# Outputs of nine chunks from ScalarE copies to a head's own half, without a drain, and a new order list

## The chip, the cores and the metric

The kernel runs on one NeuronCore of a Trainium2 chip. The metric is the device time of one execution in microseconds (us). Five engines work side by side, each through its own queue in order: TensorE (PE in the profile; its weight loads are PEld), VectorE (DVE), ScalarE (ACT), GpSimd (POOL) and SyncE (SP), whose queue issues nearly all DMAs here. They meet at semaphores.

## The reference

Two blocks follow each other. The first is a delta rule over a sequence, per batch and head; the second a feed-forward product of three matrices.

```python
B, H, S, D = 4, 8, 768, 48
k_n = k / (norm(k) + 1e-6)
for t in range(S):
    y[:, :, t] = einsum('bhd,bhde->bhe', q[:, :, t], state)
    v_old = einsum('bhde,bhd->bhe', state, k_n[:, :, t])
    state = state + beta_t * einsum('bhd,bhe->bhde', k_n[:, :, t], v[:, :, t] - v_old)
x = y.transpose(0, 2, 1, 3).reshape(B * S, H * D)      # 3072 x 384
out = (((x @ w1) * (x @ w2)) @ w3) @ w_out             # 384 -> 1024 -> 1024 -> 384
```

All of it is computed in fp32; the weights come in as 64-bit numbers and are converted on the chip.

## The kernel before

**The first block in chunks.** The 768 steps are cut into 12 chunks of 64 tokens. Two batches lie in the two halves of the 128 partitions (z = 0, 1), the other two in r = 0, 1; heads come in even and odd (e = h % 2). For a chunk m the steps are:

- `p`, `d` (or `K`, `Q` for chunks 0 and 1): keys and queries with features on the partitions, in the tile KQ; an even head's features lie in partitions 0 to 47, an odd head's in 64 to 111.
- `s`, scores, per r (a "half" of the scores): products of keys with keys and queries into a pair of PSUM banks, ps_w. VectorE takes the key part as U; the query part becomes PT, by a ScalarE copy and a GpSimd mask (chunks 0, 1 and 4 to 11), or by one VectorE product (chunks 2 and 3).
- `u`, `V`, `e`: the triangular inverse of U, for two chunks at a time. `V` is 31 steps of two VectorE operations each, with its matrix held in one pair of PSUM banks; before and behind it stand copies or DMAs, and `e` puts the corner block in.
- `c`, the chain: state times keys (from chunk 1 on), vtok minus that, the inverse times vtok, then X on VectorE (L685), then the new state S. Only this part is sequential from chunk to chunk.
- `y`, outputs: state times queries plus X times PT in one pair of PSUM banks, eight ScalarE copies into xT (L765), and every second chunk DMAs within xT.

In X and PT the data of head h and batch half z lie in partition half (z + h) % 2: odd heads are crossed. So the scores put an odd head's query part into the other half than its key part, with two products of 64 columns (L387), where an even head has one of 128 (L381). The outputs run in two modes: state products of z = 0 and all X times PT products, then `pe.drain()`, then state products of z = 1. The PSUM bank of a product is (h + z) % 2.

**The second block.** Per pair of chunks (u = 0 to 5) the feed-forward products run as `a h i j` (L988, for pair 0 `a b` at L869), sums on GpSimd (`G`, `S`), and the last product as `o` with results `x` (L1098, L1128 to L1135, stores at L1115). w3 and w_out are multiplied together at the start (`t`, `f`), after each weight piece is loaded and converted (`P`: DMA, ScalarE, VectorE, GpSimd).

**Buffers.** `two_banks()` hands out the two pairs of ps_w in turn; while an inverse `V` holds one, every other user gets the other. Tag "o" has two buffers, which the squares of the keys (`g`) and the result tiles (osb) take in turn.

**Order.** Each part is a generator and each `yield` a step. ORDER is a list of some 1,460 names written out by hand; every occurrence of a name runs that part's next step. The instructions of each engine keep the order in which they were emitted, so the list fixes all five queues.

Of the kernel before, what the change touches and what calls it, by code (L numbers as in the profile page):

```python
# [39 lines left out]
V0 P0 k0 beta P18 P13 P0 P18 P0 P0 P11 g0 P13 K0 P18 K0 P11 P18 P10 P13 P13 q0 P3 P3 P11 g0 beta  # L40
beta K0 K0 K0 k1 K1 P10 P11 P12 P3 P12 g0 g0 Q0 P10 g0 g0 g0 g0 g0 P8 Q0 Q0 Q0 K1 K1 K1 Q0 K1 P3
N0 P9 k2 P8 P8 P10 s0 P8 N0 g1 s0 s0 s0 s0 s0 s0 u0 q1 P2 Q1 P9 p2 P2 P12 P12 P9 Q1 g1 Q1 Q1 P2
u0 g1 Q1 d2 d2 u0 P5 P1 t0 t0 t5 t5 P9 t2 t2 P4 P6 s1 s1 P5 P5 P2 s1 P1 s1 s1 s1 u1 g1 P1 u1 u1
t4 V0 V0 P5 V0 V0 P4 t10 P7 P4 t3 t3 V0 V0 P1 f1 P6 P6 t4 V0 P7 V0 V0 t10 t1 P14 P7 P4 V0 f0 V0
P6 P16 P16 V0 V0 P7 t1 s0 P19 P19 P19 P19 V0 f1 P17 k3 p2 v1 V0 V0 P14 P14 P14 V0 f2 P17 f2 f0 V0
f2 P15 v0 P20 f1 t11 f0 P17 P17 f5 V0 V0 P16 t11 P16 t8 P15 V1 V0 t8 f5 t9 V0 V0 t6 P15 V0 n0 n0
f5 V0 V0 V0 V0 t9 P20 P20 V0 t6 P22 P22 P22 f4 P23 P23 V0 f4 f4 P21 P21 P15 t7 t7 V0 s1 V0 V0 V0
V0 g1 d2 d2 P22 f3 f3 P24 P20 g1 g1 p3 g1 P26 p3 P30 e0 e0 e0 t12 t14 e1 e1 g1 f3 e0 e0 d3 d3 N1
s2 s2 s2 P23 P23 t12 e0 f6 e0 p4 s2 P24 e1 e1 t14 s2 e0 P24 s2 P25 c0 P26 f7 u2 P30 P24 c0 e1 e1
P21 P21 d3 d3 y0 y0 P26 P26 P31 t15 t13 s3 s3 s3 s3 s3 s3 t13 c0 n1 n1 P32 t15 u2 u2 u3 c0 P30 f7  # L50
e1 P25 P25 P31 P31 P27 c1 c1 u3 u3 f6 e1 c1 V1 V1 V1 y0 P31 f6 f7 P25 P27 V1 V1 V1 V1 P30 b1 c1
N1 b1 v2 P32 V1 V1 P27 V1 s1 y1 y1 b2 V1 d4 V1 V1 P28 P29 P32 b2 P27 V2 V1 V1 V1 y1 b3 V1 V1 P28
P28 b0 P32 c1 b2 b2 b3 b1 b1 b0 P29 P29 b0 P29 a03 a03 a02 V1 b0 V1 d4 V1 V1 a01 V1 P28 V1 V1 a02
V1 P35 a01 a00 a00 n2 n2 a04 a04 b7 P33 P33 a05 a05 P34 P34 a01 a07 b7 V1 b4 b5 V1 V1 V1 V1 k4
a01 a07 k5 b5 b3 g2 b4 V1 V1 P35 V1 V1 g2 c1 e2 e2 e2 e2 a06 a06 g2 e3 e3 e3 b3 g2 g2 a00 a02 a02
p4 v3 d4 d4 p5 a00 e2 P34 c2 c2 e2 P34 e2 b6 P35 P35 e2 c2 c2 e3 a03 g2 g2 P33 b6 y2 g2 P33 g2 d5
d5 p5 c2 c2 y2 a04 e3 s4 N2 e3 s4 a03 s4 b6 b6 s4 s4 s4 s4 T e3 T T d5 n3 d5 a04 e3 b4 b4 b7 s5
n3 k6 g3 u4 s5 s5 s5 s5 s5 s5 b5 b7 b5 a05 T c3 c3 a06 a05 a06 u5 V2 p6 g3 a07 a07 c3 c3 g3 S0 S0
S0 V2 g3 V2 V2 N2 oD0 y3 y3 V2 V2 W oA0 S0 S0 V2 V2 S0 S0 S0 c3 v5 n5 V2 V2 S0 S0 S0 S0 V2 v4 oB0
V2 V2 V2 xA0 V2 V2 xB0 V2 V2 oA0 S0 S0 S0 n4 oB0 xA0 d6 y3 k7 xA0 V2 n4 oC0 V2 V2 V2 a10 xB0 S0  # L60
V2 V2 xC0 G1 V2 xD0 a10 a10 V2 oC0 a10 a10 d6 xC0 xC0 xC0 xD0 V2 V2 i10 V2 h10 c3 c4 V2 V2 j10 V2
V2 V2 a10 h10 i10 a12 V2 V2 h10 W W a12 p6 V2 a12 a12 j12 e4 g3 g3 h10 c4 a12 h10 a12 h12 d6 d6
s5 i12 e4 e4 e4 i10 h12 h12 g3 g3 p7 g3 e4 e4 h12 N3 s4 h12 a11 a11 a11 s6 s6 i12 i12 e5 c4 j11
s6 c4 y4 y4 c4 e5 d7 d7 h11 c4 c5 a11 p7 e5 s6 a11 a11 h11 i11 i11 n5 c5 d7 d7 N3 a13 h11 h11 e5
W e5 s7 e5 a13 s7 s7 s7 s7 s7 s7 a13 a13 s6 s6 c5 i11 k8 u7 u6 g4 g4 g4 S1 V3 V3 c5 p8 h11 s6 g4
h13 a13 j13 a13 i13 h13 i13 i13 S1 h13 V3 h13 h13 V3 V3 y5 V3 V3 V3 V3 V3 V3 d8 V3 V3 V3 y5 oC1
oA1 S1 oD1 S1 S1 V3 V3 S1 xA1 c5 oA1 xA1 oB1 v6 y5 v7 a20 a20 V3 xA1 V3 V3 V3 d8 G2 V3 V3 xB1 n6
V3 V3 V3 V3 oB1 xB1 xC1 S1 j20 k9 V3 xD1 V3 V3 V3 V3 S1 oC1 a20 a20 p8 xC1 V3 xC1 h20 V3 xD1 xC1
V3 V3 V3 V3 a20 a20 i20 h20 a22 h20 g4 c5 g4 g4 g4 a22 V3 j22 d8 h20 h20 e6 i20 g4 a22 d8 a22 h22
a22 a22 i22 e6 V4 e6 c6 i20 h22 e6 i22 h22 n7 h22 e6 e6 a21 a21 a21 n6 c6 p9 c6 s8 i22 N4 h21 h22  # L70
i21 a21 s8 a21 s6 c6 y6 s8 s8 j21 s8 v8 a21 h21 i21 y6 d9 d9 e7 p9 e7 s8 s8 e7 e7 s7 h21 h21 i21
h21 a23 c6 c6 e7 a23 i23 a23 n8 n8 d9 e7 S2 N4 d9 a23 s9 s9 s9 s9 s9 n7 s9 k10 s9 u8 g5 a23 a23
c7 c7 h23 h23 i23 i23 c7 c7 g5 u9 h23 h23 V4 V4 V4 j23 h23 S2 g5 g5 V4 V4 V4 V4 p10 v9 V4 y7 y7
V4 V4 oA2 V4 V4 d10 V4 y7 V4 V4 S2 oD2 S2 d10 xA2 V4 S2 S2 oB2 oC2 V4 c7 xB2 V4 V4 V4 V4 oB2 xB2
xC2 xD2 p10 V4 V4 V4 oA2 V4 V4 a30 a30 G3 a30 a30 S2 S2 oC2 k11 V4 xC2 j30 s9 V4 xD2 xC2 V4 V4 V4
V4 V4 V4 xA2 xA2 xC2 g5 a30 h30 a30 i30 a32 h30 V4 V4 V4 e8 h30 i30 c7 a32 j32 h30 h30 g5 a32 a32
i32 g5 g5 d10 d10 i30 a32 a32 e8 h32 h32 i32 p11 e8 e8 a31 a31 c8 e8 s8 c8 g5 a31 j31 e8 c8 n9 c8
h32 h32 h32 y8 y8 c8 e9 e9 i31 d11 d11 h31 e9 e9 n9 a31 c8 s10 a31 p11 i32 N5 s10 s10 a31 h31 s10
s10 s10 s10 c9 c9 h31 e9 e9 d11 d11 u10 i31 i31 s11 a33 a33 S3 a33 v11 h31 h31 s11 s11 s11 s11
s11 a33 c9 i33 a33 a33 c9 h33 h33 s11 u11 i33 i33 j33 h33 h33 V5 V5 V5 V5 y9 S3 h33 V5 V5 V5 v10  # L80
n10 n10 oA3 S3 S3 V5 V5 oD3 V5 oB3 s10 y9 y9 oC3 V5 V5 S3 S3 V5 V5 V5 V5 V5 xA3 xB3 V5 V5 n11 V5
V5 oB3 V5 xB3 xD3 xC3 xC3 xD3 oA3 G4 a40 S3 S3 a40 a40 V5 oC3 N5 V5 V5 V5 xA3 a40 a40 xC3 h40 a40
h40 i40 V5 V5 V5 V5 h40 h40 V5 j40 h40 i40 V5 V5 V5 V5 a42 a42 a42 a42 i42 h42 a42 j42 xA3 V5 V5
a42 i40 h42 i42 h42 h42 a41 a41 a41 a41 h41 a41 V5 e10 e10 e10 e10 h42 n11 a41 i42 h41 i41 i41
i41 h41 e10 e11 h41 e10 c9 j41 a43 a43 a43 S4 c9 e11 e11 e11 h41 c10 c10 h43 c10 a43 e11 j43 xC3
a43 c10 a43 i43 h43 i43 i43 h43 h43 e11 h43 c10 c10 y10 y10 c11 s11 oD4 c11 c11 c11 oA4 xA4 y11
S4 S4 S4 oB4 oA4 y11 y11 S4 S4 S4 xA4 xB4 oB4 xB4 oC4 xC4 xA4 a50 xC4 S4 oC4 xC4 xD4 xD4 a50 G5
a50 h50 a50 a50 i50 a50 h50 i50 i50 h50 h50 j50 h50 a52 a52 a52 a52 i52 a52 a52 h52 a51 h52 i52
j52 h52 h52 h52 i51 a51 a51 a51 h51 i52 S5 a51 a51 h51 i51 j51 h51 h51 i51 a53 a53 a53 a53 h53
a53 a53 h53 j53 h51 h53 h53 h53 i53 i53 i53 xC4 o5 x5 o5 S5 S5 o5 o5 x5 S5 S5 S5 S5 o5 x5 x5 o5  # L90
x5 x5 x5 x5 x5 x5 S5 o5 x5 x5 x5 x5
# [4 lines left out]
def kernel(  # L96
# [14 lines left out]
    P = 128  # L111
# [258 lines left out]

    def scores(m):
        u = Us[m % 2][:, 0 : NR * H * C].rearrange("p (r h t) -> p r h t", r=NR, h=H)
        for r in range(NR):
            KQ = KQs[m]
            ps = two_banks()
            for h in range(H):
                for z in range(2):
                    x = KQ[feat(h % 2), NR * z + r, h // 2]
                    n = 128 * (h // 2)
                    if h % 2 == 0:  # L380
                        pe.matmul(  # L381
                            ps[half(z), 0, n : n + 128], lhsT=x[:, 0, :],
                            rhs=x.rearrange("p j t -> p (j t)"), start=True, stop=True,
                        )
                    else:
                        for j in range(2):
                            pe.matmul(  # L387
                                ps[half(z ^ j), 1, n + C * j : n + C * j + C],
                                lhsT=x[:, 0, :], rhs=x[:, j, :], start=True, stop=True,
                            )  # L390
# [13 lines left out]
            if m < 2 or m > 3:  # L404
                act.copy(out=by_parity(PT), in_=psv[:, :, :, 1, :])  # L405
                yield
                pool.tensor_tensor(  # L407
                    out=PT, in0=PT, in1=smask[:].unsqueeze(1).to_broadcast([P, H, C]), op=ALU.mult
                )
            else:  # L410
                dve.tensor_tensor(
                    out=by_parity(PT), in0=psv[:, :, :, 1, :],
                    in1=smask[:].unsqueeze(1).unsqueeze(1).to_broadcast([P, NP, 2, C]),
                    op=ALU.mult,
                )
# [295 lines left out]
    def outputs(c):  # L711
        PT, St, X, KQ = PTs[c], Ss.get(c), Xs[c], KQs[c]
        py = two_banks()
        pyv = py[:].rearrange("p x (b a t) -> p x b a t", b=B, a=2)

        def region(h, z, r):
            return pyv[feat(h // NP), (h + z) % 2, NR * z + r, h % NP // 2, :]
# [5 lines left out]
        for mode, todo in enumerate(modes):  # L723
# [8 lines left out]
            for r in range(NR if mode == 0 else 0):  # L732
                for a in range(NP):
                    for h in (a, NP + a):
                        for z in range(2):
                            x = half((z + h) % 2)
                            todo.append((h, z, r, X[x, r, h, :], PT[x, r, h, :]))
        part = [(h // NP, (h + z) % 2) for todo in modes for h, z, *_ in todo]
        issued, n = ([], []), 0
        for mode, todo in enumerate(modes):  # L740
            if mode:
                drain = pe.drain().ins
# [7 lines left out]
        for i in issued[0]:  # L750
# [8 lines left out]
        for z in range(2):  # L759
# [528 lines left out]
```

## Time and profile before

| | us |
|---|---|
| median of 3 runs | 557.11 |
| the runs | 554.81, 557.11, 559.89 |
| the profiled execution | 556.14 |
| its span, first to last instruction | 554.1 |
| TensorE's mean granted clock | 0.997 |
| VectorE operations of a pair's X (L685), mean | 0.952 |
| TensorE waiting for DMA of ktok, total | 15.3 |
| ScalarE waiting for the outputs' products, total | 44.0 |

A page of the profile shows busy time of each engine, then the span in slices, the DMA queues, the chain of waits followed back from the last instruction, and the costliest groups of instructions (engine, operation, tile written and read, partitions x elements). Matmuls are pipelined and their ends are modelled; start times say more than durations. An fp32 product shows as two instructions.

### The profile page before, as it was taken

Reading aid. Unit: us, or ns where it says so; the run is one execution under the profiler, and the core shown is the slowest. Engines: PE = TensorE matmul, PEld = TensorE weight load, DVE = VectorE, ACT = ScalarE, POOL = GpSimd, SP = SyncE. Lnnn points to the kernel's source line nnn. Section 1 sums busy time; section 2 is a strip of 40 time slices with the busy share of each in tenths; the row PEclk is TensorE's granted clock in tenths of the full one; section 3 lists DMA queues with packets and bytes.
Section 4 is the critical chain, followed back from the end, with each engine's and each line's share of the span. In section 5 each row is a group of like instructions: output and inputs, shape, how many; then the busy total and the mean of one; then the engine's idle time right before and its main releaser. Section 6 shows DMA issues by size and latency. Waiting matters only on the chain.

```text
span 554.1 us, 19883 instructions
## 1 busy us (share of the span) xinstructions
PE 520.0 (94%) x8540; PEld 446.7 (81%) x8540; DVE 388.0 (70%) x850; ACT 188.1 (34%) x393; POOL 256.6 (46%) x278
## 2 busy tenths in 40 slices
PE   2486998999999999999999999999999999999997
PEld 2473566688778988889988889988899888998897
DVE  3889999899876878659977579859587654123332
ACT  3688388954542112332022430123221121300000
POOL 8576473723659970455443355510482212342141
PEclk9998999999999999999999999999999999999999
DMA  8986987579457345455553564253411220020001
GB/s 247 197 200 211 161 224 126 138 157 151 63 80 128 76 110 82 60 100 89 99 108 64 82 120 76 92 83 46 106 31 44 63 50 2 10 66 1 0 1 57
DMA packets 197687, 52.64 MB, mean 95 GB/s; under 512 B 185344, under 2 KB 191488, under 8 KB 197600
## 3 DMA queue, kind: packets, MB, share of 16 engines
q1 hardware_dynamic: 193408, 50.59, 44.8%
q10 hardware_dynamic: 4192, 0.79, 1.0%
q8 instruction: 67, 1.10, 0.8%
q14 instruction: 20, 0.16, 0.1%
HBM read 41.25 MB, written 8.91 MB: 91 GB/s over the span
## 4 chain that ended last, share of the span: by engine, by line
PE 74%; DVE 4%; ACT 1%; issue 1%; DVEq 0%
PE ps_f L988 35%; PE ps_f L1098 19%; PE ps_w L645 5%; PE ps_w L744 4%; PE ps_f L869 4%; PE ps_w L574 2%; PE ps_w L381 1%; PE ps_w L387 1%; DVE ps_w L487 1%; DVE tb L482 1%; ACT TT L547 1%; PE ps_w L1098 1%; DVE KQ L337 0%; DVE ab L885 0%; DVE Ub L501 0%
## 5 line engine op out<-in xcount | busy, mean ns | idle before, releaser
L996 DVE TENSOR_TENSOR ab<-ab,ps_f 128x512 f32<-128x512 f32 x80 | 54.5, 682 | 58.5 <-PE ps_f L988 57.8
L1069 POOL TENSOR_TENSOR ab<-ab 128x512 f32<-128x512 f32 (+1 forms) x56 | 61.4, 1118 | 41.5 <-PE ps_f L1098 24.4
L988 PE MATMUL ps_f<-xT,w1s 128*128 128x256 f32 x320 | 78.5, 382 | 0.0
L1035 POOL TENSOR_TENSOR ab<-ab,late 128x512 f32<-128x512 f32 x19 | 24.2, 1272 | 107.6 <-DVE ab L996 106.1
L988 PEld LDWEIGHTS ps_f<-xT,w1s 128*128 128x128 f32 x320 | 59.9, 190 | 7.9
L1098 PE MATMUL ps_f<-w,ab 128*128 128x192 f32 x376 | 65.5, 328 | 0.0
L1098 PEld LDWEIGHTS ps_f<-w,ab 128*128 128x128 f32 x376 | 61.3, 190 | 1.3 <-issue 0.5
L849 PE MATMUL ps_f<-w2s,w3T 128*128 128x384 f32 x128 | 45.3, 505 | 4.9 <-POOL w2s L805 4.9
L407 POOL TENSOR_TENSOR PT<-PT,smask 128x512 f32<-128x512 f32 x20 | 25.6, 1283 | 50.9 <-ACT PT L405 50.9
L1098 PE MATMUL ps_f<-room,ab 128*128 128x192 f32 x272 | 47.2, 328 | 0.0
L498 DVE TENSOR_TENSOR ps_w<-ps_w,tb 128x31 f32<-128x31 f32 (+15 forms) x124 | 43.3, 349 | 4.2
L765 ACT COPY xT<-ps_w 48x256 f32<-48x256 f32 x96 | 30.5, 366 | 44.5 <-PE ps_w L744 44.0
L1098 PEld LDWEIGHTS ps_f<-room,ab 128*128 128x128 f32 x272 | 44.3, 190 | 0.6 <-issue 0.3
L493 DVE TENSOR_TENSOR tb<-ps_w,Ub 128x31 f32<-128x31 f32 (+15 forms) x124 | 41.9, 338 | 3.6 <-ACT ps_w L473 0.3
L1004 ACT COPY ab<-ps_f 128x512 f32<-128x512 f32 x20 | 11.7, 585 | 95.1 <-PE ps_f L988 95.0
L988 PE MATMUL ps_f<-xT,room 128*128 128x256 f32 x160 | 41.1, 384 | 0.0
L849 PEld LDWEIGHTS ps_f<-w2s,w3T 128*128 128x128 f32 x128 | 24.0, 194 | 20.4 <-POOL w2s L805 5.5
L988 PE MATMUL ps_f<-xT,w2s 128*128 128x256 f32 x160 | 40.1, 381 | 0.0
L988 PE MATMUL ps_f<-x_room,w2s 128*128 128x256 f32 x160 | 38.9, 386 | 0.0
L988 PEld LDWEIGHTS ps_f<-x_room,w2s 128*128 128x128 f32 x160 | 29.5, 190 | 5.2 <-DVE late L996 1.0
L988 PEld LDWEIGHTS ps_f<-xT,w2s 128*128 128x128 f32 x160 | 30.1, 190 | 4.1
L988 PEld LDWEIGHTS ps_f<-xT,room 128*128 128x128 f32 x160 | 29.6, 190 | 4.7 <-DVE osb L1128 0.6
(146 smaller groups left out, 1005.5 us busy)
## 6 DMA issues: line engine op xcount, KB each, us to landing
raw<-in_moe_w_dram SPq DMA_DIRECT2D x16, 512.0 KB, 5.6
vtok<-in_v_dram SPq DMA_DIRECT2D x24, 192.0 KB, 4.5
raw<-in_moe_w_dram SPq DMA_DIRECT2D x24, 192.0 KB, 4.6
out_dram<-osb SPq DMA_DIRECT2D x46, 96.0 KB, 1.7
ktok<-in_k_dram SPq DMA_DIRECT2D x44, 96.0 KB, 3.4
raw<-in_moe_w_out_dram SPq DMA_DIRECT2D x8, 384.0 KB, 4.2
perm<-in_k_dram SPq DMA_DIRECT2D x40, 64.0 KB, 3.0
perm<-in_q_dram SPq DMA_DIRECT2D x32, 64.0 KB, 2.6
```

Source lines behind the costliest of these rows:

```text
L407: pool.tensor_tensor(out=PT, in0=PT, in1=smask[:].unsqueeze(1).to_broadcast([P, H, C]), op=ALU.mult)
L493: dve.tensor_tensor(out=tv, in0=V[:, 0 : s + 1, s : s + 1].to_broadcast([P, s + 1, n]), in1=U[:, s, s + 1 : BS].unsqueeze(1).to_broadcast( ...
L498: dve.tensor_tensor(out=o, in0=o, in1=tv, op=ALU.subtract)
L645: pe.matmul(out(ps, r, h, z), lhsT=lhs(r, h, z), rhs=rhs(r, h, z), start=True, stop=True,)
L744: i = pe.matmul(region(h, z, r), lhsT=lhs, rhs=rhs, start=part[n] not in part[:n], stop=part[n] not in part[n + 1 :],)
L765: act.copy(out=xT[f, p:NP:2, b : b + NR, cc, :].rearrange("p a r t -> p r a t"), in_=pyv[f, z, b : b + NR],)
L849: pe.matmul(ps[:, 0:DM], lhsT=w3Ts[jc, kc // 4][:, kc % 4 * P : kc % 4 * P + P], rhs=wo[:, kc], start=(kc == 0), stop=(kc == KF - 1),)
L988: pe.matmul(acc[name][:, n * i : n * i + n], lhsT=ws[b][:, P * i : P * i + P], rhs=xs[x], start=new and k == 0 and i == 0, stop=k == len(t ...
L996: dve.tensor_tensor(out=o_, in0=x, in1=acc[name], op=ALU.add)
L1035: eng.tensor_tensor(out=Z1, in0=Z1, in1=late, op=ALU.mult)
L1069: pool.tensor_tensor(out=o_, in0=x_, in1=y_, op=op)
L1098: pe.matmul(ps[b][:, b, :], lhsT=block(u, HF * f + i, z)[:, P * b : P * b + P], rhs=ws_[w][:, i], start=first and i == 0 and (b == 0 or n ...
```

## The change

SWAPPED names nine chunks: 1 and 4 to 11, those with a state whose PT is made by ScalarE. For them:

- scores: an odd head has one product of 128 columns, like an even one; its query part stays in the half of its batch. Per half of the scores, 8 products of 128 columns and 16 of 64 become 16 of 128.
- PT: four ScalarE copies of 64x256 per half in place of one of 128x512; they move each head to the half of its own parity (e) and each batch half to its own slots.
- outputs: a new first step makes Xc, X with its halves crossed, by two ScalarE copies of 64x384 into a buffer of tag "o". The products of head h then read partition half h % 2 of X (z = 0) or Xc (z = 1), and write bank h % 2. All products form one mode, with no drain between them.
- evictions into xT: four copies of 48x512 in place of eight of 48x256.

Chunks 0, 2 and 3 stay as they are. ORDER has one more `y` step for each of the nine chunks and is otherwise the same steps, in a new order behind the first nine.

```diff
 ORDER = """
-V0 P0 k0 beta P18 P13 P0 P18 P0 P0 P11 g0 P13 K0 P18 K0 P11 P18 P10 P13 P13 q0 P3 P3 P11 g0 beta
-beta K0 K0 K0 k1 K1 P10 P11 P12 P3 P12 g0 g0 Q0 P10 g0 g0 g0 g0 g0 P8 Q0 Q0 Q0 K1 K1 K1 Q0 K1 P3
...
+V0 P0 k0 beta P18 P13 P0 P18 P0 P18 P0 P18 P11 g0 P10 q0 P3 P11 P11 P11 k1 P13 P13 P13 P12 P10 P3
+P8 g0 g0 P9 K0 K0 K0 K0 K0 P3 P10 Q0 Q0 Q0 Q0 Q0 P3 k2 g0 g0 P12 g0 g0 g0 g0 K1 beta K1 P10 s0
...
+i30 h32 j31 N5 e8 c8 c8 y8 h32 i32 h32 i32 y8 y8 a31 a31 e9 i31 N5 h32 c8 e9 d11 d11 p11 e9 c8
...
 """
+    SWAPPED = (1, *range(4, NCH))
...
-                    if h % 2 == 0:
+                    if h % 2 == 0 or m in SWAPPED:
                         pe.matmul(
-                            ps[half(z), 0, n : n + 128], lhsT=x[:, 0, :],
+                            ps[half(z), h % 2, n : n + 128], lhsT=x[:, 0, :],
...
-                act.copy(out=by_parity(PT), in_=psv[:, :, :, 1, :])
+                if m in SWAPPED:
+                    for z in range(2):
+                        for e in range(2):
+                            act.copy(
+                                out=PT[half(e), NP * z : NP * z + NP, :],
+                                in_=psv[half(z), :, e, 1, :],
+                            )
+                else:
+                    act.copy(out=by_parity(PT), in_=psv[:, :, :, 1, :])
...
+        swapped = c in SWAPPED
+        if swapped:
+            Xc = in_turn(ffn, [P, NR * NP, D], "o", 2, "Xc")
+            for e in range(2):
+                act.copy(
+                    out=Xc[half(e)].rearrange("p (r a) d -> p r a d", r=NR),
+                    in_=X[half(1 - e)].rearrange("p r (a e) d -> p r a e d", e=2)[:, :, :, e],
+                )
+            yield
...
-            return pyv[feat(h // NP), (h + z) % 2, NR * z + r, h % NP // 2, :]
+            return pyv[feat(h // NP), (h if swapped else h + z) % 2, NR * z + r, h % NP // 2, :]
...
-        for mode, todo in enumerate(modes):
+        for mode in range(2):
+            todo = modes[0 if swapped else mode]
...
+            for r in range(NR if mode == 0 and swapped else 0):
+                for a in range(0, NP, 2):
+                    for z in range(2):
+                        for h in (a, a + 1, NP + a, NP + a + 1):
+                            x = half(h % 2)
+                            todo.append((
+                                h, z, r, Xc[x, NP * r + h // 2, :] if z else X[x, r, h, :],
+                                PT[x, r, NP * z + h // 2, :],
+                            ))
...
-            if mode:
+            if mode and todo:
                 drain = pe.drain().ins
...
-        for i in issued[0]:
+        for i in issued[0] if issued[1] else ():
             in_order(i, drain)
...
-        for z in range(2):
+        for e in range(2):
+            f = feat(e)
+            for p in range(2 if swapped else 0):
+                act.copy(
+                    out=xT[f, p:NP:2, :, cc, :].rearrange("p a b t -> p b a t"), in_=pyv[f, p]
+                )
+        for z in range(0 if swapped else 2):
```

## The prediction

> **What bounds the kernel now.** I read the page's busy shares first, then five windows, then TensorE's waits, then the timeline of one chunk's outputs and of its scores. The windows' columns are the stretch, its length, then busy us and instructions of PE, PEld, DVE, ACT, POOL, granted clock, DMA share, GB/s.
>
> ```profile
> PE 520.0 (94%) x8540; PEld 446.7 (81%) x8540; DVE 388.0 (70%) x850; ACT 188.1 (34%) x393; POOL 256.6 (46%) x278
> ```
>
> ```profile
> 0.00:40.00 40.00, 21.42 (x481) 18.80 (x482) 27.49 (x50) 25.49 (x47) 29.00 (x42) 1.00 0.89 212
> 40.00:140.00 100.00, 92.10 (x1256) 66.34 (x1255) 93.09 (x221) 70.18 (x135) 50.30 (x49) 0.98 0.79 169
> 140.00:160.00 20.00, 17.96 (x685) 14.93 (x685) 17.34 (x41) 10.79 (x24) 9.41 (x13) 1.00 0.39 51
> 160.00:360.00 200.00, 199.10 (x3419) 177.35 (x3407) 153.60 (x353) 47.88 (x112) 108.98 (x122) 1.00 0.50 93
> 360.00:554.00 194.00, 189.41 (x2726) 169.25 (x2724) 96.46 (x187) 33.73 (x78) 58.94 (x55) 1.00 0.19 40
> ```
>
> There are two regimes. From 0 to 40 the DMA engines are 0.89 busy, and from 40 to 140 VectorE is the fullest engine (93.1 of 100); the chain of waits runs through its two-operation steps of the second inverse until 138.9. From 160 on TensorE is the bound: of 394 us it is idle 5.5, and 3.8 of that is the final drain of results behind its last product. ScalarE is at 21% there. A microsecond of TensorE work removed after 160 should therefore come off the end; work put on ScalarE costs only where TensorE must wait for it.
>
> ```profile
> 249.18 0.66 PE L744 MATMUL ps_w<-KQ,S 48*48 48x64 f32 x32
> 249.66 1.08 PE L744 MATMUL ps_w<-PT,X 64*48 64x64 f32 x64
> 250.86 0.66 PE L744 MATMUL ps_w<-KQ,S 48*48 48x64 f32 x32
> 251.45 5.47 PE L1098 MATMUL ps_f<-w,ab 128*128 128x192 f32 x32
> ```
>
> This is one chunk's outputs (start, us, instructions; each fp32 product shows as two). The 32 state instructions ahead of the attention ones take 0.48 from start to next start; the same 32 behind the drain take 0.59, and they start only when the last attention product has ended, at 250.74, plus 0.12.
>
> **Part by part, TensorE.** Outputs: 2.27 us now (249.18 to 251.45). Without the drain the three groups follow each other at their own pitch: 0.48 + 64 x 15.3 ns = 0.98 + 0.48 = 1.94 (the pitch is that of the 64 attention weight loads, which take 0.98 together in chunk 11). That frees 0.33; the lower bound is the visible hole alone, 0.12. I take 0.30, near the upper end, since the pipe's filling again (0.59 against 0.48) goes too. Eight of the nine chunks (4 to 11) have their outputs after 160: 2.4 us, bounds 1.0 to 2.6. Chunk 1 lies in VectorE's regime and counts nothing.
>
> Scores: an odd head's two 64-column products become one of 128, so a half goes from 48 instructions to 32.
>
> ```profile
> 239.13 0.33 PE L381 MATMUL ps_w<-KQ 48*64 48x128 f32 x2
> 239.14 0.33 PE L387 MATMUL ps_w<-KQ 48*64 48x64 f32 x4
> ...
> 239.95 0.28 PE L387 MATMUL ps_w<-KQ 48*64 48x64 f32 x3
> 240.05 0.24 PE L645 MATMUL ps_w<-vtok,TT 64*64 64x48 f32 x2
> ```
>
> From this half's first product to the next work behind it: 0.92 us; two other halves show 0.94. The columns stay the same. The large products take 0.166 us for 192 columns (32 instructions from 251.45 to 256.75), so 128 columns take 0.11; with the four array quarters working side by side, 32 instructions need 8 x 0.11 = 0.88. That leaves 0.04 to 0.06 to gain. If instead the count of instructions set the pace (0.93/48 = 19 ns), 16 fewer would free 0.31. Bounds 0 and 0.31; I take 0.06, by the column pace, which even heads already set. Sixteen halves (chunks 4 to 11): 1.0 us, bounds 0 to 5.
>
> **ScalarE.** Each half's copy of PT (585 ns, row below) becomes four of 64x256. The nearest rows are 128x256 at 369 and 48x256 at 366; eight of the latter in a row took 2.59, so four take about 1.3: 0.7 more per half, 18 halves, 13 us. Xc is new: two copies of 64x384 per chunk; 128x384 out of PSUM takes 479, a copy within SBUF with long strides takes 1.09 for 512 elements a row, 0.82 for 384. X is read in runs of 48, nearer the first: 0.96 a chunk, 1.6 at worst, 9 to 15 us in all. The evictions into xT go from eight (2.59) to four of 48x512 (579 each): 2.3, or 2.6 us less in nine chunks. Net +19 us on 188. From 160 on ScalarE idles 312 of 394 us, so as throughput this costs nothing; as latency it has three places.
>
> ```profile
> L405 ACT COPY PT<-ps_w 128x512 f32<-128x512 f32 x20 | 11.7, 585 | 25.5 <-DVE U L393 25.5
> L765 ACT COPY xT<-ps_w 48x256 f32<-48x256 f32 x96 | 30.5, 366 | 44.5 <-PE ps_w L744 44.0
> L685 DVE TENSOR_TENSOR X<-ps_w,wt x12: 945/950/957, 92.3 to 475.1; 128x768 f32<-128x768 f32 x12
> ```
>
> First, outputs now wait for Xc, and all of TensorE's queue waits behind them. From the end of the products that X is made of: X 0.95, Xc 0.96, three hand-overs of about 0.1, so 2.2. I added up the products that the new list puts between the two, by the chain's durations: 3.0 us for chunk 1, then 2.6, 7.8, 2.6, 3.5, 1.7, 3.5, 14.9, 2.7 for chunks 4 to 11. The state products and the uncrossed pairs, which need no Xc, cover 0.6 more. Only chunk 8 is tight (1.7 + 0.6 against 2.2): cost 0. With the long-stride price (+0.7) chunk 8 alone loses 0.6. Behind Xc on ScalarE stand that chunk's own evictions, for chunk 7 the two copies that open an inverse, for chunk 10 one copy of a product's A, none due at once.
>
> Second, Xc takes a turn of the two buffers of tag "o". In the new list it follows a results buffer only in chunks 10 and 11, whose stores are issued 9 or more steps ahead; stores land in 1.7 us (issues of out_dram). Cost 0; one missed would be 2.
>
> Third, a score's ps_w pair is held for U (0.69) and the copies (now 1.3), with hand-overs 2.2 instead of 1.4, and while an inverse holds the other pair the next chain, score or output product waits for it. Adding up TensorE work between successive users of a pair in the new list, after 160 chunk 7's two score halves (ahead of chunk 6's second half and of chunk 5's chain) are short by 0.5 each, 1.0 in all. The old list is short by 0.3 to 0.45 in four places there, 1.5, three of them outputs, whose eviction gets shorter. The trace shows TensorE idle for 1.7 in all between 160 and 550, so some of that did not happen. Net 0, bounds -1 to +2.
>
> A page of the Trainium skill speaks against this change: TensorEngine Tiling (Array Packing), Performance Considerations, PSUM Bottleneck, says that packing small products speeds up TensorE but not the emptying of PSUM, which may then become the bound. This trace bears it out little so far (TensorE idle 1.7 us from 160 to 550); by it the time would be that of the first rival.
>
> **The list.** Behind the first nine steps all is reordered. Ahead of the second inverse's last step both lists ask VectorE for the same 33 weight pieces, 65 inverse steps, 12 score and 10 transposition steps; the new one has one chain step more and one 0.35 us step fewer. So VectorE's regime should end at the same time, about 139, unless its 19 us of idle time before 140 change. The new list issues q0 and k1 earlier (15th and 20th step, before 21st and 31st) and the second steps of beta later. Ahead of the first product that needs that inverse it has about 2.2 us less of TensorE work (86.5 against 88.7), which is left for later; against that stand 2.0 us of idle TensorE in 140 to 160 that it may fill. I take +0.5, bounds -4 to +5, the width from VectorE's idle time.
>
> **Sum.** -2.4 - 1.0 + 0 + 0.5 = -2.9. The profiled execution took 556.14 (span 554.1 and 2.0 around it): 553.2. The median of the runs, 557.11, lies 1.0 above it: 554.2.
>
> **Rivals.** About 1% (5.6 us) is what a measurement can tell from no change: the three runs spread over 5.1. So faster is below 551.5, slower above 562.7.
>
> *ScalarE's longer eviction sets the pace (slower).* If the 0.7 us more were exposed at all 16 score halves, 11.2 less 2.9: 565.4. It decides where the work between two users of a pair is under 2.2 us while the other pair is held. For: chunk 7. Against: most places have more, and ScalarE's idle share. Chance 0.12.
>
> *The new beginning loses.* VectorE gets to the end of the second inverse 4 us later, because its weight pieces or beta arrive in another order: 558, between 556 and 562. For: DMA at 0.89 before 40. Chance 0.22.
>
> *The new beginning gains, or instruction count paces the scores.* Earlier k1 removes part of TensorE's 15.3 us of waits for ktok and 4 us of VectorE's idle time, or scores free 5: 549.5. Against: VectorE's work is unchanged. Chance 0.20.
>
> *The drain was hardly in the way.* Its hole alone goes, scores gain nothing: 557.1 - 1.0 + 0.5 = 556.6. Chance 0.10.
>
> **How the numbers follow.** The forecast has 0.36, 552 to 556. Of the gaining rival nearly all and a little of the forecast lies below 551.5: faster 0.22. The first rival and a few hundredths of the second lie above 562.7: slower 0.14. Same 0.64. The range 549 to 561.5 leaves out most of the first rival and the gaining rival's tail.
>
> **What would show it.** Right: no hole in the outputs, about 1.95 us from their first product to the next work; score halves of 0.88; TensorE's busy time about 3 us less; no waits on Xc above 0.5. Wrong: TensorE waiting for ScalarE's PT or Xc copies by more than 3 us after 160; the second inverse ending more than 3 us from 138.9; or outputs at 2.2 us in spite of the missing drain.

## The result, and the profile after

The changed kernel takes 563.38 us (median of four runs, 561.64 to 564.21), the kernel before beside it 557.52 (554.81 to 559.89): ratio 1.0119, interval 1.0087 to 1.0151. It became slower by 5.9 us, where 554.2 was forecast, and the time lies outside the range. The profiled execution's span went from 554.1 to 562.5.

The page's busy shares and the windows of the changed kernel (columns as before):

```profile
PE 523.8 (93%) x8252; PEld 447.1 (79%) x8252; DVE 389.6 (69%) x850; ACT 209.1 (37%) x429; POOL 256.0 (46%) x278
```

```profile
0.00:40.00 40.00, 16.84 (x376) 14.49 (x378) 24.16 (x46) 22.57 (x41) 25.75 (x39) 1.00 0.90 197
40.00:140.00 100.00, 90.53 (x1339) 64.38 (x1340) 90.00 (x203) 68.38 (x131) 48.16 (x47) 0.95 0.71 161
140.00:160.00 20.00, 20.00 (x303) 16.79 (x304) 17.04 (x38) 12.70 (x23) 12.63 (x15) 1.00 0.68 96
160.00:360.00 200.00, 197.74 (x3545) 174.02 (x3537) 154.59 (x360) 64.06 (x151) 107.08 (x121) 1.00 0.49 88
360.00:562.00 202.00, 198.65 (x2708) 177.37 (x2708) 103.84 (x207) 41.39 (x85) 62.38 (x58) 1.00 0.21 45
```

Two rows show where the time went. From 0 to 40 TensorE does 376 products in place of 481: everything starts later. From 160 on it is as full as before. Over the whole span it is busy for 3.8 us more, with 288 recorded products fewer.

The timeline of one chunk's outputs after (start, us, what), then of two score halves in a row, first before and then after:

```profile
233.02 0.66 PE L777 MATMUL ps_w<-KQ,S 48*48 48x64 f32 x32
233.51 0.29 PE L777 MATMUL ps_w<-PT,X 64*48 64x64 f32 x8
233.62 0.29 PE L777 MATMUL ps_w<-PT,Xc 64*48 64x64 f32 x8
...
234.40 0.63 PE L777 MATMUL ps_w<-KQ,S 48*48 48x64 f32 x32
234.85 1.09 PE L657 MATMUL ps_w<-X,ktok 64*64 64x48 f32 x64
```

```profile
163.11 0.33 PE L381 MATMUL ps_w<-KQ 48*64 48x128 f32 x2
163.12 0.33 PE L387 MATMUL ps_w<-KQ 48*64 48x64 f32 x4
...
165.13 1.13 PE L869 MATMUL ps_f<-xT,w2s 128*128 128x256 f32 x4
```

```profile
245.72 1.98 PE L385 MATMUL ps_w<-KQ 48*64 48x128 f32 x64
247.63 1.13 PE L1027 MATMUL ps_f<-xT,spare 128*128 128x256 f32 x4
```

The outputs have no hole. From their first product to the next work they take 1.83 us here, where the chain's small products follow, and 1.94 where large ones do; with the drain it was 2.16 and 2.27. Two score halves in a row with large products behind them take 1.91 us (247.63 - 245.72) against 2.02 (165.13 - 163.11), or 0.955 a half against 1.01: 16 instructions fewer bring 0.055. The 0.92 and 0.94 in the prediction belong to halves with small products behind them, which begin while the half's last products run, and can't be compared with these.

The end of an inverse is VectorE's transposition of it. Both inverses, before (line 501) and after (line 513):

```profile
78.17 1.25 DVE L501 STREAM_TRANSPOSE Ub<-ps_w 128x1024 f32<-128x1024 f32 x1
...
137.65 1.25 DVE L501 STREAM_TRANSPOSE Ub<-ps_w 128x1024 f32<-128x1024 f32 x1
```

```profile
82.88 1.25 DVE L513 STREAM_TRANSPOSE Ub<-ps_w 128x1024 f32<-128x1024 f32 x1
...
146.81 1.25 DVE L513 STREAM_TRANSPOSE Ub<-ps_w 128x1024 f32<-128x1024 f32 x1
```

The second inverse's starts at 146.81 and ends at 148.06; before, it started at 137.65 and ended at 138.9. The first inverse's starts at 82.88 against 78.17. So 4.7 us are lost ahead of 83 and 4.4 more up to 147. From chunk 3's X (181.57 after, 173.0 before) to the end of the span both kernels take the same, 380.9 and 381.1.

And in the changed kernel's chain of waits there is something that the prediction had not looked at:

```profile
95.51 0.61 PE ps_w L657 x39
96.12 1.39 issue
97.51 0.56 PE ps_w L657 x19
```

In the midst of one group of products TensorE stands still for 1.39 us and waits for nothing that the profile shows.

### The profile page after: what moved, and what is told of

It is laid out like the page before. It is cut to its first block, busy times and chain, and to the rows that moved or that the text cites. A ratio compares the mean times of both kernels' runs of the same rounds, so it can differ in the third digit from the quotient of the medians.

```text
span 562.5 us, 19376 instructions
## 1 busy us (share of the span) xinstructions
PE 523.8 (93%) x8252; PEld 447.1 (79%) x8252; DVE 389.6 (69%) x850; ACT 209.1 (37%) x429; POOL 256.0 (46%) x278
## 4 chain that ended last, share of the span: by engine, by line
PE 82%; ACT 6%; DMA 4%; DVE 4%; issue 2%; SPq 2%; POOL 0%; DVEq 0%; ACTq 0%; POOLq 0%
PE ps_f L1027 35%; PE ps_f L1137 19%; PE ps_f L888 8%; PE ps_w L657 6%; PE ps_f L908 4%; PE ps_w L777 4%; DMA X<-in_q_dram 3%; PE ps_w L385 3%; PE ps_w L586 2%; ACT PT L412 1%; ACT columns L456 1%; DMA raw<-in_moe_w_dram 1%; ACT xT L804 1%; PE ps_w L1137 1%; DVE tb L494 1%
## 5 line engine op out<-in xcount | busy, mean ns | idle before, releaser
L888 PE MATMUL ps_f<-w2s,w3T 128*128 128x384 f32 x128 | 47.7, 528 | 5.7 <-ACT w3T L882 5.7
L1043 ACT COPY ab<-ps_f 128x512 f32<-128x512 f32 x20 | 11.7, 586 | 87.7 <-PE ps_f L1027 86.8
L888 PEld LDWEIGHTS ps_f<-w2s,w3T 128*128 128x128 f32 x128 | 25.3, 204 | 22.4 <-ACT w3T L882 6.1
L844 POOL TENSOR_TENSOR w<-w,raw 128x512 uint32<-128x512 uint32 x16 | 20.9, 1308 | 34.9 <-DVE w L840 18.0
L283 POOL TENSOR_TENSOR sq<-ktok 128x384 f32<-128x384 f32 x24 | 20.6, 864 | 31.0 <-DMA ktok<-in_k_dram 24.8
```

What stands on the lines that cost most here:

```text
L888: pe.matmul(ps[:, 0:DM], lhsT=w3Ts[jc, kc // 4][:, kc % 4 * P : kc % 4 * P + P], rhs=wo[:, kc], start=(kc == 0), stop=(kc == KF - 1),)
```

## The experiments

All ratios are to the kernel before, run in the same job. The expectations name the theories: A, the new list's beginning loses; B, the new code loses (ScalarE's later PT and Xc); C, TensorE's instructions come in blocks, and what matters is where a block ends; E, the order of beta, K1 and Q0 at the start; F, what stands behind the early q0 on ScalarE and VectorE.

**Code and list apart.** *code_old_list*: the new code in the old ORDER, each of the nine new steps put behind its chunk's X. *list_old_code*: the old code in the new ORDER without those steps.

```diff
 (code of after, ORDER of before; one of nine places)
-e5 c4 j11 s6 c4 y4 y4 c4 e5 d7 d7
+e5 c4 j11 s6 c4 y4 y4 y4 c4 e5 d7 d7
```

> The changed code (nine chunks, Xc, no drain) in the order of the kernel before; each of the nine Xc steps stands right behind the step that makes X. Theory A, the new list loses the time and the code gains what the prediction said: 552 to 556, with the second inverse ending at 139 to 141 and outputs of 1.94 us. Rival B, the code itself loses it through ScalarE's longer copies: 560 to 566.

> The code of the kernel before in the new list, without the nine Xc steps. Theory A: 564 to 568, slower than the changed kernel (563.4), since the drains come back on top of the list's loss. Rival B: 555 to 559, as before.

Measured: 568.82, ratio 1.0206 (1.0176 to 1.0236), and 564.92, ratio 1.0142 (1.0109 to 1.0175). The code alone is slower than either theory had it; the list alone falls where theory A put it. Either half of the change loses by itself, and both together (1.0119) lose less than the code alone. No sum of two separate costs does that. The new code's trace in the old list has stops like the one above at eight places, 8.4 us in sum; the old code's in the new list has none, the kernel before one of 0.35. The timeline of three of them (in brackets the idle time ahead and its releaser):

```profile
92.27 0.56 PE L656 MATMUL ps_w<-vtok,TT 64*64 64x48 f32 x22 [1.43 <-issue]
97.63 0.66 PE L776 MATMUL ps_w<-PT,X 64*48 64x64 f32 x30 [0.81 <-issue]
...
387.18 0.55 PE L656 MATMUL ps_w<-X,ktok 64*64 64x48 f32 x24 [1.55 <-issue]
```

I counted TensorE's recorded instructions (products and weight loads) ahead of each: 1709, 1964, 2218, 3997, 4252, 11611, 12120, 15167. Neighbours differ by 254 or 255, the others by multiples of 253.8 to 254.5. That is a grid of 256 instructions, less one or two that leave no record. The page's table of DMA queues shows what has this size:

```profile
q8 instruction: 67, 1.10, 0.8%
```

This is the kernel before: 67 packets of 16.4 KB for 17,080 recorded instructions, one for 255. The changed kernel has 16,504 and 65 packets.

The traces also hold the time of each packet of this queue. In the 18 kernels of this document 55 stops of over 0.25 us stand on the grid, and every one of them ends 1.26 to 1.76 us after such a packet has landed. The packet itself takes 0.88 to 1.98 us, and of 1,190 pairs of neighbouring packets none start less than 3.28 us apart. So on the grid TensorE waits for its instructions, and they come no faster than a block in some 3.3 us. Eleven more stops of the same look are not on the grid. One of 0.36 to 0.47 us, for instance, stands at the same product (line 657 in the changed kernel, at 250.74) in seven kernels and moves with it when products are added ahead; what holds TensorE there is open.

**The list's beginning.** *head101* and *head766*: the new code, the first 101 or 766 steps in the old order and the rest in the new one.

```diff
 (ORDER of after)
-V0 P0 k0 beta P18 P13 P0 P18 P0 P18 P0 P18 P11 g0 P10 q0 P3 ...
+V0 P0 k0 beta P18 P13 P0 P18 P0 P0 P11 g0 P13 K0 P18 K0 P11 ...
```

> The changed code; the first 101 steps of the list (up to the end of chunk 1's scores, about the first 42 us) in the order of before, all others in the new order. Theory A1, the loss begins with the order of the first loads and of the products up to the first score (3 to 5 us late there, and more behind it through the clock and the interleaving): 553 to 558. Rival A2, the loss is made later, between 45 and 150 us, where the new list mixes weight pieces and the inverses differently: 559 to 563.

> The changed code; the first 766 steps (to about 245 us; there both lists have done exactly the same steps) in the order of before, the rest in the new order. Theory A, the rest of the new list is as good as the old one: within 2 us of the changed code in the old list, 552 to 557. Rival A3, the new list also loses in the part that TensorE bounds: 3 us or more above the changed code in the old list.

Measured: 559.7, ratio 1.0032 (1.0012 to 1.0052), and 562.13, ratio 1.0077 (1.0049 to 1.0105). With the old first 101 steps alone most of the loss comes back: 3.7 us by the medians, 4.8 by the two ratios, each to the kernel before of its own job. It is less than theory A1 hoped for, since the time stays above 558. The first inverse's transposition stands at 78.72 again and the second's at 142.58, so what is lost between the two remains. The first holds in all traces: it starts at 77.1 to 81.1 in the 13 kernels with the old beginning and at 81.7 to 84.4 in the 5 with the new one. More of the old list makes it worse, which neither expectation had: head766 has four stops (1.17, 1.07, 0.87, 0.73) at other places than head101's (1.27 and 0.27 on the grid, 0.68 and 0.47 off it).

**Moving the blocks.** Small products that nobody uses, ahead of the first step, while TensorE waits for its first data: 32 of them are 128 instructions, half a block; 64 are 256, a whole one.

```diff
+    for _ in range(4):
+        ps = bank([P, 512])
+        for i in range(8):
+            z = i % 2
+            pe.matmul(ps[half(z), 0:16], lhsT=ident[half(z), half(z)], rhs=ident[half(z), 0:16], start=True, stop=True)
     for name in ORDER.split():
         step(name)
```

> The changed code in the old list, with 32 small products ahead of everything (128 more TensorE instructions, done while TensorE waits for its first keys). In the run without them TensorE stopped 8.4 us in all in the midst of groups, waiting for nothing that the profile shows, each time 254 to 255 recorded instructions (or a multiple) behind the stop before. Theory C, the stops stand where a block of 256 instructions ends inside a dense run of small products and the next block has not come yet: the shift by half a block puts the ends elsewhere, so the stops move by 128 instructions and their sum changes; most likely it falls to 0 to 4 us, and the time by as much, 562 to 567. Rival D, they belong to places in the kernel (a queue, a semaphore): the same products stop, 8 us, 567 to 571.

> As the run before with 64 products, 256 instructions: a whole block. Theory C: the ends of blocks fall on the same products as without any, so the stops are where they were and sum to 6 to 10 us, 567 to 571. It is also the control for the added products themselves: if they alone changed something, both shifted runs would differ from the run without.

> The kernel before, shifted by 128 instructions. Its one stop of 0.35 us stands on the same grid. Theory C: the few stops there are the luck of where the ends of blocks fall, so the shift brings 1 to 6 us of stops and 558 to 563. Rival D, or a cause in the changed code (denser outputs): no stops, 556 to 559.

> The control to the kernel before with 128 instructions more ahead (ratio 1.0245): now 256 more, so that every later product stands at its old place within a block of 256. Theory C: the stops are again those of before (one, near 469, of 0.35 us), and the time is that of before, ratio 0.997 to 1.004. Rival: added products ahead cost time by themselves, at the beginning or through the clock; then it is at least as slow as with 128, ratio 1.024 or more.

> The changed kernel with 128 instructions of TensorE more ahead. Theory C: the two stops of 0.40 and 1.39 us behind 90 go, and others come: in the trace of the changed kernel, blocks of 256 counted half a block further along would take less than 3.4 us each at a number of places, in sum 8.0 us less, against 3.2 for the blocks as they stand (of which 1.8 to 2.3 show as stops). So some 4 to 5 us slower than the changed kernel: about 568, ratio to before 1.016 to 1.024. Rival: the changed kernel's loss is all in its list's beginning and the places of the blocks don't matter for it: 563 to 564, ratio 1.010 to 1.013.

| kernel | median, us | ratio (interval) | stops over 0.25 us, sum |
|---|---|---|---|
| new code, old list, 0 / 128 / 256 | 568.82 / 566.61 / 568.07 | 1.0206 / 1.0147 (1.0108 to 1.0186) / 1.0191 (1.0154 to 1.0228) | 8.4 / 5.0 / 6.3 |
| before, 128 | 570.58 | 1.0245 (1.0198 to 1.0291) | 9.7 |
| before, 256 | 556.04 | 1.0008 (0.9987 to 1.0029) | 0 |
| after, 128 | 568.37 | 1.0212 (1.0176 to 1.0248) | 7.3 |

The kernel before, with nothing changed but half a block of idle instructions ahead, loses 12.7 us, more than twice the most that was expected; with a whole block it is itself again. This excludes that the added products themselves cost the time (the granted clock was 0.991 and 0.988 in the two profiled executions). The stops of over 0.25 us are 9.7 of the 11.7 us between the profiled spans. A whole block under code_old_list brings five of its eight stops back, at the same products (those at 377, 387 and 481 us again stand at lines 585, 656 and 776; the first and third also come back, the other three do not). Half a block moves them, and leaves more than the 0 to 4 us expected. Of after_shift128's 7.3 us, 1.2 are two stops off the grid. In the shifted kernel before, two of eleven:

```profile
236.22 0.27 PE L574 MATMUL ps_w<-T,U 33*33 33x32 f32 x9 [2.04 <-issue]
...
470.98 0.31 PE L574 MATMUL ps_w<-T,T 33*33 33x32 f32 x14 [1.32 <-issue]
```

From the counts one can take how long TensorE needed for the block that ends in a stop. Of the blocks behind 160 in the ten kernels run so far, 22 took 3.2 us or less, and 12 of these end in a stop; of 447 longer ones 8 do, four of them one or two blocks behind a short one. For eleven of the twelve, block and stop together come to 3.0 to 3.8 us. The twelfth, the 0.35 of the kernel before, comes to 2.4, and the largest stop, the 2.04 above, stands behind a block of 3.79 (the expectation of before_tail below has none behind a block over 3.7): there the block's packet started 3.4 us after the block before had ended, and 0.2 to 1.5 us after it for the eleven. So a short block is nearly a condition, but not enough. What spares the other ten, and why a packet starts late, is open.

**The stop by itself.** *before_tail*: behind the last product of the kernel before, 256 idle products of 64x16 and 256 of 64x128 over two quarters of the array. *before_tail4*: 512 of 64x16 over all four.

```diff
     for name in ORDER.split():
         step(name)
+    for _ in range(4):
+        ps = two_banks()
+        for i in range(128):
+            z, y = i % 2, i // 2 % 2
+            pe.matmul(ps[half(y), z, 0:16], lhsT=ident[half(z), half(z)], rhs=ident[half(z), 0:16], start=True, stop=True)
```

> The kernel before with a tail that nobody uses, issued by TensorE behind its last product: 256 products of 64x16 and then 256 of 64x128 (64 contracted, fp32). It measures the disputed stop by itself. Theory C, sharpened: a block of 256 instructions takes about 3.3 to 3.6 us to come in, and TensorE stops at its end for what is left of that (in the shifted kernels block time and stop come to 1.87+1.55, 1.91+1.33, 2.24+1.16, 2.42+1.20 us; no block over 3.7 us had a stop). Then the part with 16 columns shows a stop at each end of 254 to 256 recorded instructions, each block with its stop 3.3 to 3.6 us long, and the part with 128 columns, whose block takes far longer than 3.6 us, shows none. Rival: the stops come from what stands at those places (a wait that the records don't show, a DMA), and a run of products that waits for nothing has none; then the 16-column part runs through at a steady pace.

> The tail again, denser, since the last one was not dense enough to tell: there a product of 64x16 over two quarters of the array took 14.6 us per 1000 recorded instructions, a block of 256 thus 3.7 us, and nothing stopped. Now 512 products of 64x16 in turn over all four quarters, behind the last product of the kernel before. The kernel's outputs in that form run 256 instructions in 1.7 to 2.2 us. Theory C (a block takes 3.3 to 3.6 us to come in): stops of 1.0 to 1.7 us at each end of 254 to 256 recorded instructions, block and stop together 3.3 to 3.6 us, 8 blocks in 27 to 29 us. Rival (the stops belong to what stands at those places): a steady pace without stops, 8 blocks in 14 to 18 us; or, if four quarters bring no more than two, 8 blocks in 30 us without stops, which would leave it open.

One execution of each was timed, 607.0 and 581.5 us, the tail included. The first missed: its first part ran at 14.6 ns an instruction, 3.7 us a block, too slow for a stop under either theory. The second, its timeline (whose first row begins with the window; the tail begins at 549.49) and two windows of it:

```profile
549.81 2.66 PE L1261 MATMUL ps_w<-ident 64*64 64x16 f32 x167
554.15 21.79 PE L1261 MATMUL ps_w<-ident 64*64 64x16 f32 x768 [1.69 <-issue]
576.35 2.11 PE L1261 MATMUL ps_w<-ident 64*64 64x16 f32 x69 [0.41 <-issue]
```

```profile
551.00:552.00 1.00, 1.00 (x84) 1.00 (x77) 0.00 (x0) 0.00 (x0) 0.00 (x0) 1.00 0.66 211
...
560.00:561.00 1.00, 1.00 (x47) 1.00 (x44) 0.00 (x0) 0.00 (x0) 0.00 (x0) 0.50 0.00 0
```

These products wait for nothing. At full clock TensorE starts 137 recorded instructions in a microsecond, a block in 1.85 us, and then stops for 1.69: 3.54 together. That is one stop alone: the tail's first block end, at 550.4, has none, and during the stop, at 553.8, the granted clock falls to 0.50. From then on a block's instructions alone need 3.3 to 3.4 us, and block ends follow each other by 3.6 to 4.0 with gaps between weight loads of 0.2 to 0.5 (counts 17967, 18479, 18735, 18991, all on the grid). The fall of the clock is not what stops TensorE: in before_tail it comes at 557.1, and no stop with it. The tail's 2,048 instructions brought 8 packets more:

```profile
q8 instruction: 75, 1.23, 0.9%
```

So a block takes about 3.5 us to come in, 3.6 to 4.0 at half the clock, and TensorE, ready earlier, waits for the rest. The Trainium skill, Runtime: NRT & Kernel Launch, section "Instruction fetch mechanics", says that an engine's instructions come in blocks of 256, the next fetched while the current one runs, and that crossing an end is "mostly hidden". The traces agree with the block and differ on the rest: 1.69 us here, 12.7 us in one kernel.

**Beta and K1 ahead of Q0.** *after_beta_k1*: in the new list beta's second and third step and K1's first are put ahead of Q0.

```diff
-K0 P3 P10 Q0 Q0 Q0 Q0 Q0 P3 k2 g0 g0 P12 g0 g0 g0 g0 K1 beta K1 P10 s0 beta
+K0 P3 P10 beta beta K1 Q0 Q0 Q0 Q0 Q0 P3 k2 g0 g0 P12 g0 g0 g0 g0 K1 P10 s0
```

> The changed kernel; in its list only the transpositions of beta and the products of K1 are put ahead of those of Q0, as they stood in the old list. Theory E, chunk 0's scores came 3.2 us late because K1 and beta stood between Q0 and them in TensorE's queue: the first U starts at 28.5 to 30 (32.3 in the changed kernel, 29.05 before) and the time falls by 2 to 4, 559.5 to 561.5. Rival F, the early load of q0 and k1 delays the weight pieces and with them VectorE: U no earlier than 31, 562.5 to 564.

Measured: 565.79, ratio 1.0137 (1.0103 to 1.017). Theory E falls: the first U comes at 33.04, later than the changed kernel's 32.28, as F had it (the time is above F's as well). What the start seems to hang on is ScalarE's queue. In the timeline of ScalarE, first the changed kernel and then head101:

```profile
8.57 1.23 ACTq L234 DMA_DIRECT2D X<-in_q_dram  x1
13.93 0.66 ACT L836 ACTIVATE w<-raw 128x512 f32<-128x512 f32 x1 [4.77 <-DMA raw<-in_moe_w_dram]
...
22.92 2.37 ACT L360 COPY KQ<-ps_f 48x512 f32<-48x512 f32 x4 [1.29 <-PE ps_f L350]
...
26.44 0.18 ACT L272 COPY ss<-ss 128x16 f32<-128x16 f32 x1
```

```profile
12.33 0.60 ACTq L233 DMA_DIRECT2D X<-in_q_dram  x1
...
21.86 0.19 ACT L271 COPY ss<-ss 128x16 f32<-128x16 f32 x1
...
22.50 3.36 ACT L359 COPY KQ<-ps_f 48x512 f32<-48x512 f32 x6
```

With q0 issued at 8 instead of 12, raw weight tiles land later (ScalarE's wait for them is 4.77), and ScalarE's copies of Q0 now stand ahead of the copies of the norms' sums, which VectorE's norms, and then U, wait for: 26.44 against 21.86, and U at 32.28 against 27.76. That order is read from the traces; it was not undone by itself.

**The number of instructions.** Three kernels keep all of the change but the single products: odd heads' scores are again two products, to the same places, so that TensorE has 17,080 instructions as before.

```diff
-                    if h % 2 == 0 or m in SWAPPED:
+                    if h % 2 and m in SWAPPED:
+                        for j in range(2):
+                            pe.matmul(ps[half(z), 1, n + C * j : n + C * j + C],
+                                      lhsT=x[:, 0, :], rhs=x[:, j, :], start=True, stop=True)
+                    elif h % 2 == 0:
```

> The new code in the old list (568.8), with one thing put back: odd heads' scores of the nine chunks as two products of 64 columns again, to the same places in PSUM, so that TensorE's instructions number what they did before (17,080 recorded) and each stands at its old place within a block of 256. Everything else of the change stays: outputs without a drain, ScalarE's two copies, PT in four copies. Theory C: the stops of 8.4 us in sum go down to 0.4 to 1.5, so 560 to 562, ratio 1.003 to 1.010, though it has 576 instructions more than its parent. Rival (ScalarE's later PT and Xc cost the new code its time in the old list): as slow as the parent, ratio 1.018 or more. If the single products saved what the prediction gave them (1.0 us), the rival's ratio goes up by 0.002.

> The changed kernel with the two products put back. Theory C: as in the old code under the new list, no stop is left of the 1.8 to 2.3 us, so 561 to 562, ratio 1.005 to 1.010. Rival (single products save time): 1.0 us slower than the changed kernel, ratio 1.013 to 1.015. If it is neither (1.010 to 1.013), the two cancel or are both nil.

> The new code with the old first 101 steps (ratio 1.0032), two products put back. Theory C: of its stops 2.0 to 2.7 us go, so 557 to 558, ratio 0.996 to 1.001; with the gain of the outputs (0.33 us in each of eight chunks) it could come out ahead of the kernel before. Rival: no stop goes, or new ones come at other places, ratio 1.003 to 1.007.

Measured: 559.54, ratio 1.0053 (1.0029 to 1.0077), in the old list; 563.06, 1.0091 (1.0059 to 1.0122), in the new one; 560.86, 1.0057 (1.0033 to 1.0081), in the mixed one. In the old list 576 instructions *more* save 8.5 us by the ratios (9.3 by the medians): of the eight stops none is left, one of 2.48 at 113 (not on the grid; its cause is open) is new. In the other two the early stops go, but one of 1.29 or 1.30 comes at 310 us, and nothing measurable is won. (head101_two's trace is that of its slowest execution, 564.09.) Theory C is right in the old list; in the mixed list it was too hopeful, since it counted only what goes.

**A better place for the blocks.** *head101_shift240*: head101 with 240 instructions ahead. By the sum of max(0, 3.4 us - time of a block) over its trace this was nearly the best of 16 shifts.

```diff
-        for i in range(8):
+        for i in range(15):
```

> The new code with the old first 101 steps (559.7) and 240 instructions of TensorE more ahead, which puts every block end 16 instructions later in the steps than it was. Theory C, worked out on that kernel's trace with 3.4 us for a block: blocks that are too short come to 2.8 us in sum, against 3.2 as they stand (other shifts: 2.7 to 11.6). So no more than 0.4 us is to be had: 559 to 560, ratio 1.000 to 1.004, with the stops of 1.27 and 0.68 us at other places. If it comes out under 0.998, a version of the new code beats the kernel before; above 1.008 the sum by blocks is no guide to the time.

Measured: 561.11, ratio 1.0092 (1.0056 to 1.0128): a miss. On the grid, stops of 1.35 and 1.33 us took the place of 1.27 and 0.27; the one of 0.68, off it, stays at its product with 0.70. The sum tells bad places (after_shift128) but not differences of a microsecond or two. No version of the new code beat the kernel before.

## Why the prediction was wrong, by its steps

- **Outputs, -2.4:** right. 1.94 us in place of 2.27, about 0.33 in each of eight chunks, -2.6; the working gave 1.94 and took 0.30.
- **Scores, -1.0:** right in the gain, 0.055 a half against 0.06, or 0.9 in sixteen halves. The level is not: a half with large products behind it takes 0.955 and not 0.88, as it took 1.01 and not 0.92 before. That after_two, with the two products back, is no slower than the changed kernel says nothing against it, since two stops go there.
- **ScalarE, 0:** nearly. Xc's copies take 0.51 each (0.96 a chunk expected, 1.02 measured) and PT's four 0.365 each (1.46 a half, 1.3 expected). TensorE's waits of over 0.25 us for anything but issue come to 1.2 us behind 160 (two, both for PT copies, none for Xc), against 0.3: about +0.9, within the bounds, and far from the first rival's 11. That this rival's time, 565.4, lies nearest to the measured one is chance. In the old list these waits are 2.7.
- **The list, +0.5:** the failed step. "VectorE's regime should end at the same time, about 139", because the same work is asked for; it ended at 148.1. With the old code and no stop at all the new list by itself costs 1.42% (list_old_code), some 8 us, above the bound of +5. Its profiled span has 8.6 us more than the kernel before: 4.0 ahead of the first inverse's end, 1.2 from there to chunk 3's X, 3.4 behind it. The second rival laid the loss to the order in which weight pieces or beta arrive and priced it at 4 at the second inverse's end, where it came to 9.2: the first 101 steps are worth 4.2 us at the first inverse's end and 3.7 to 4.8 in the time. Counting VectorE's operations could not show it. By the traces, though not by an experiment of its own, what moved was ScalarE's order at 8 to 27 us, where VectorE has idle time. That q0 and k1 are issued earlier was seen, but weighed only in the gaining rival.
- **TensorE busy 3 us less** (a sign): 3.8 more. Much of it is the clock: one group of eight fold products takes 5.42 us at 51, and 2.74 at full clock; 0.50 is granted from 49.4 to 56.2, and 0.69 on the mean from 50 to 60.
- **What no term held:** the stops at block ends. The change takes 576 instructions out of TensorE's stream, so every later product stands elsewhere in its block. Before, one end brought a stop (0.35 us); in the changed kernel two do, at 91 and 97.5 (0.40 and 1.39). The prediction priced instructions by their pace only.

The span's 8.4 us, as far as they are placed: 4.7 ahead of the first inverse's end; 3.9 from there to chunk 3's X; then -0.2. For the 3.9 there are the two stops (1.8), a wait for a PT copy at 172.7 (0.8) and at most 1.7 for a granted clock of 0.83 in 110 to 120 (it was 1.00 before). They come to more than 3.9, so how it divides is open. list_old_code, which has none of the three, loses 1.2 there. Whether the new list brings on that clock dip was not tried; after_shift128, with the same list, has none there. The -0.2 is what is left when the outputs (-2.6) and twelve score halves (-0.7) have won back what the new list costs behind chunk 3's X, 3.4 with the old code. Some 1.2 of that is work: five recorded feed-forward products of pair 0, which the old list has done by then. The rest is not placed. The 2.5 us between the span's difference and that of the medians is the spread of single executions.

So the right account of the time is the second rival, with a list that also costs behind its beginning, plus a mechanism that nobody had named. The new list hides it: it suits the new number of instructions (1.8 us of stops on the grid) as the old list suits the old number (0.35), while the new code in the old list loses 8.4.

## What to carry to other kernels

Where TensorE runs series of small products at under 14 ns an instruction, look for a second floor of about 3.5 us for each block of 256. It is one for blocks in a row; of single short blocks about half had no stop here. Count the instructions ahead of an "issue" stop in the chain of waits, look whether the counts differ by multiples of about 254, and whether a packet of the instruction queue landed about 1.4 us ahead of the stop's end. A shift of half a block by idle products ahead of everything, with a whole block as its control, tells in two runs whether a kernel's time hangs on it; an edit that removes instructions must be judged under more than one shift, or its gain and the blocks' luck can't be told apart. And ahead of a kernel's first heavy stage, compare the order in each queue, ScalarE's as well, not the amount of work.

## What was not expected of the hardware

- A block of 256 of TensorE's instructions took 3.54 us at full clock in a run of products that wait for nothing (1.85 issuing, 1.69 stopped), and 3.6 to 4.0 at clock 0.50: the fetch does not double its time when the granted clock halves.
- A stop at a block's end ended 1.26 to 1.76 us after the landing of a packet of 16.4 KB on the instruction queue, 55 times out of 55, and two such packets never started less than 3.28 us apart.
- 128 idle instructions at the start of the kernel before cost 2.45% (1.98 to 2.91), 256 cost 0.08% (-0.13 to 0.29).
- In both tails the granted clock fell to 0.50 within 4 to 6 us of the first of the small products, and stayed there for 20 us or more.
- A weight load and product of 64x16 over two quarters of the array take 14.6 ns an instruction, over four 7.3.
